# Squared-ReLU attention and a routed expert layer on one core: expert weights gathered at set blocks, and turned token rows written from another ring of buffers

## The chip, the cores and the metric

The kernel runs on one core of a Trainium2 chip. The metric is the time of one execution in device microseconds (us); a kernel's time is the median of its runs. A core has five engines that each work through a queue of their own, strictly in order: TensorE (PE, matmuls), VectorE (DVE), ScalarE (ACT), GpSimd (POOL) and SyncE (SP). They wait for one another through semaphores. SP and POOL also issue the transfers between device memory and the core's buffers; a gather or a scatter through a list of indices is issued by POOL.

## The reference

`u`, `v` are 8 x 2496 x 256, `z` is 8 x 2496 x 64, all of it f32. Attention has a squared ReLU in place of a softmax, and its result gates `u`; each of the 19968 tokens then goes to one of 8 experts.

```python
scores = scale * np.matmul(z, z.transpose(0, 2, 1))     # scale = 1 / 2496
attn = np.maximum(scores, 0.0) ** 2
x = (u * np.matmul(attn, v)).reshape(19968, 256)

logits = x @ w_gate                                     # 256 x 8
expert_idx = np.argmax(logits, axis=1)
gate_w = softmax(logits)[expert_idx]                    # of the chosen expert
for e in range(8):
    mask = expert_idx == e
    h = np.maximum(x[mask] @ w1[e], 0.0)                # 256 x 1024
    out[mask] = gate_w[mask, None] * (h @ w2[e])        # 1024 x 256
```

## The kernel before

**Precision.** A product of f32 operands is made of three matmuls: each operand is split into a rounded part ("hi", a cast on ACT) and a residual ("lo", a subtraction on DVE).

**Attention.** A step is (batch b, chunk c of up to 512 queries, pair kp of two blocks of 128 keys). `scores` (L311) runs three steps ahead: it makes the two key blocks' scores, squares them (L339, L340) into a buffer of the ring `tf` (`ring_f`, 3 buffers), casts (L319, L343) and subtracts (L320, L345, L349, L350). Scores that another chunk has in transposed form are read from there (L319, L320, and for half a chunk L335 to L338, through the buffers `rows`). `weighted` (L366, L368, L369) multiplies them with `v` into `acc0` and `acc1`. At a chunk's end `gate_x` (L383) multiplies by `u` and splits the result in three for the gate (L392 to L395); `turn_rows` transposes it (L407, into a buffer of the ring `th`, `ring_halves`, 3 buffers) and writes it out as token rows (L412); `route` (L438) finds each token's expert and its place in the expert's list (the products L471 and L473, then L480 to L487), and scatters entries there (L490, four per chunk).

**Expert tiles.** Tiles are counted from 0. The first eight ("A", 512 tokens each) take tokens of all batches but the last; two of them share the weights of an expert (`NA` = 4 pairs). The others are built from the rest of the lists. Weights are called (w, h): expert set w, half h, 1 MB each, gathered by `load_w` (L712) through an index column into one of six slots s0 to s5. One half holds two "pieces" (two blocks of the 1024 hidden features each), which `split_piece` (L746) turns into hi and lo: two casts on ACT (L762, L764) and two subtractions on DVE (L763, L765) a piece. The next steps for a tile i are

- `load_x` (L743): POOL gathers its token rows, 128 rows a gather, into a buffer of the ring `rows` (3 buffers);
- `turn_x` (L768): DVE transposes 32 x 32 squares of it into `sq` (L773), SP writes that to memory (L776, `far`) and reads it back with features on the partitions into `tp` (L778); `sq` and `tp` are both buffers of the ring `th`, and `sq` comes free when L776 has landed;
- `split_x` (L782): the cast L788 and the residual L789;
- per block of 128 hidden features `up` (six matmuls L809, then L813 on ACT and L814 on DVE) and `down` (six matmuls L835 to L837), eight blocks a tile; `up` runs two blocks ahead of `down`;
- `turn_y` (L850) transposes the result back, `finish` (L872) multiplies by the gate into a buffer of the ring `tf` (L879) and POOL scatters the rows to the output (L886).

**What sets the order.** The last batch's last chunks already start the expert tiles: the table `loads` names, by the number of steps left, what is issued there. In `tiles` (L1038) a tile's block 0 loads what comes later: the second half of the next set and the first half of the one after it, and the rows of tile i + 3; its middle block turns tile i + 2. The program's text is not the order on the engines. A scheduler places every instruction by a simulated timeline, as soon as it finds its operands and buffers free; only what is issued through `pinned` (L373) is put behind the instruction that was last issued on each engine. What is placed early in an engine's queue holds up all that stands behind it there.

Of the kernel before, what the change touches and what calls it, by code (L numbers as in the profile page):

```python
# [8 lines left out]
F32 = mybir.dt.float32  # L9
# [3 lines left out]
I32 = mybir.dt.int32  # L13
# [6 lines left out]
P = 128  # L20
KQ = 64
G, R = 4, 32
D = 256
# [31 lines left out]
def fused_kernel(ctx: ExitStack, tc: tile.TileContext, zt, ut, v, wg, wcat, out):  # L55
    nc = tc.nc
    B, _, SP = zt.shape
    S = SP - KQ
    NK = SP // P
    NKP = NK // 2  # L60
# [7 lines left out]
    NA = 4  # L68
# [10 lines left out]
    sb = ctx.enter_context(tc.tile_pool(name="sb", bufs=1))  # L79
# [8 lines left out]
    def ring_f():  # L88
        return sb.tile([P, 2, QC], F32, name="tf", tag="tf", bufs=3)
# [13 lines left out]
    def ring_halves():  # L103
        return sb.tile([P, 4, QC], U16, name="th", tag="th", bufs=3)
# [5 lines left out]
    def slot(i):  # L110
        return sb.tile([P, 2 * F], F32, name=f"s{i}", tag=f"s{i}")
# [157 lines left out]
    def turn(b, c, cc, h, a):  # L269
# [3 lines left out]
        else:  # L273
            tt = turned_.pop((b, c, cc))
        to = tt.rearrange("p (s t i k) -> p i t s k", s=G, t=4, i=4)[:, 2 * h:2 * h + 2]
        nc.vector.transpose(out=to, in_=a.rearrange("p i (t s k) -> p i t s k", t=4, s=G))  # L276
        if h:
# [3 lines left out]
    def bring(b, cc, c):  # L281

        d = kept_rows.pop((b, cc, c))
        st = slot(home["bring", b, cc, c])
        for q in range(G):
            nc.sync.dma_start(st[q * R:(q + 1) * R].rearrange("p (g e) -> p g e", g=G),
                              d.rearrange("(g q) (s e) -> s q g e", g=G, s=G)[q])
        brought[b, cc, c] = st.rearrange("p (g t i k) -> p t i g k", g=G, t=4, i=4)
# [84 lines left out]
    def pinned(work):  # L373

        last = {}
        for i in nc.cur_bb.bb.instructions[-400:]:
            last[i.engine] = i
        with ExitStack() as behind:
            for i in last.values():
                behind.enter_context(tc.issue_after(i))  # L380
            work()
# [296 lines left out]
    NF = F // P  # L678
# [18 lines left out]
    own = [t not in seconds[which] for which, t, _ in order]  # L697
    wof = [sum(own[:i + 1]) - 1 for i in range(NT)]
# [6 lines left out]
    lists, ents, xgs, pieces, turned, xts, yts = {}, {}, {}, {}, {}, {}, {}  # L705
    outs, kept = [], []

    def load_w(w, h):
        which, t, _ = order[first_of[w]]
        wr = slot(free[0])  # L710
        free.append(free.pop(0))
        nc.gpsimd.indirect_dma_start(out=wr, out_offset=None, in_=wcat,  # L712
                                     in_offset=bass.IndirectOffsetOnAxis(ap=lists[which]["widx"][:, h, t:t + 1], axis=0))
        weights[w, h] = wr

    by2, by4 = [lst.rearrange("(a k) w -> a (k w)", k=k) for k in (2, 4)]
# [1 line left out]
    def load_e(i):  # L718
        which, t, n = order[i]
        en = ents[i] = sb.tile([P, BS, ENT], F32, name="ent", bufs=9)  # L720
        to = en.rearrange("p s w -> p (s w)")
        eidx = lists[which]["eidx"]
        parts = [(by4, t, 0, BS)] if n == BIG else [(by2, t, 0, 2)]
        for s in range(2, blocks[i] if n < BIG else 0):
            parts.append((lst, lists[which][{384: 2, 448: 4, 480: 5}[n], s / 2] + t, s, s + 1))
        for src, at, a, z in parts:
            d = nc.gpsimd.indirect_dma_start(out=to[:, a * ENT:z * ENT], out_offset=None, in_=src,
                                             in_offset=bass.IndirectOffsetOnAxis(ap=eidx[:, at:at + 1], axis=0))
            if which == "A":
                firsts.append(d)  # L730
                for of, o in scatters:
                    if of == B - 1:
                        tc.declare_no_dep(d.ins, o.ins, reason="places of a later batch")
# [4 lines left out]
    def load_x(i):  # L738
        which, k = order[i][0], blocks[i]
        src = xrows[0:NTOK - S, :] if which == "A" else xrows  # L740
        xg = ring_rows()
        for s in range(k):
            nc.gpsimd.indirect_dma_start(out=xg[:, s, :], out_offset=None, in_=src, in_offset=token(i, s))  # L743
        xgs[i] = xg
# [23 lines left out]
    def turn_x(i):  # L768

        k = blocks[i]  # L770
        xg = xgs.pop(i)
        sq, tp = [ring_halves().rearrange("p a n -> p (a n)").bitcast(F32)[:, 0:k * D] for _ in range(2)]
        nc.vector.transpose(out=sq.rearrange("p (g i s t) -> p s g i t", g=G, i=2, s=k),  # L773
                            in_=xg[:, 0:k, :].rearrange("p s (g i d) -> p s g i d", g=G, i=2))
        far = dram.tile([P, F], F32, name="far", tag="far", bufs=4)
        nc.sync.dma_start(far[:, 0:k * D], sq)  # L776
        for g in range(G):
            nc.sync.dma_start(tp[g * R:(g + 1) * R].rearrange("p (a e) -> p a e", a=G),  # L778
                              far[:, g * k * 2 * R:(g + 1) * k * 2 * R].rearrange("(a p) e -> p a e", a=G))
        turned[i] = tp  # L780

    def split_x(i):  # L782

        k = blocks[i]
        tp = turned.pop(i).rearrange("p (a j t) -> p j a t", a=G, t=R)
        xh, xl = [x.rearrange("p i n -> p (i n)")[:, 0:k * D] for x in (ring_hi(), ring_lo())]
        h, l = [x.rearrange("p (j a t) -> p j a t", a=G, t=R) for x in (xh, xl)]
        nc.scalar.copy(h, tp)  # L788
        nc.vector.tensor_tensor(l, tp, h.bitcast(F32), op=ALU.subtract)  # L789
        xts[i] = [x.rearrange("p (i n) -> p i n", i=2) for x in (xh, xl)]  # L790

    def flat(i):
        return cols[i] != SMALL and i < NM - 3

    def up(gi):
        i, g = groups[gi]
        n = cols[i]
        w1 = pieces[piece_of[gi]][0]
        xh, xl = xts[i]
        ph = ps1.tile([P, QC], F32, name="ph", tag="ps1")  # L800
        m = fs_of[i]
        for c in range(m):
            f = g * m + c
            fs = slice(f % 2 * P, (f % 2 + 1) * P)
            o = ph[:, c * n:(c + 1) * n]
            p = 0
            for dd in range(2):
                for part, xx in ((0, xh), (0, xl), (1, xh)):
                    nc.tensor.matmul(o, lhsT=w1[:, part, dd, fs], rhs=xx[:, dd, :n], start=p == 0, stop=p == 5)  # L809
                    p += 1  # L810
        hh, hl = ring2(), ring2()
        m *= n
        nc.scalar.activation(hh[:, :m], ph[:, :m], AF.Relu)  # L813
        nc.vector.scalar_tensor_tensor(hl[:, :m], ph[:, :m], 0.0, hh[:, :m].bitcast(F32),  # L814
                                                     op0=ALU.max, op1=ALU.subtract)
        return hh, hl
# [150 lines left out]
    for work in (lambda: split_v(0, 0), lambda: split_z(0, 1), lambda: split_z(0, 2), lambda: prepare(0),  # L967
# [8 lines left out]
             NKP + 1: [lambda: load_w(0, 0)],  # L976
             NKP: [lambda: load_x(1)],
             NKP - 1: [lambda: load_w(0, 1)],
             NKP - 3: [lambda: load_w(1, 0)],
             NKP - 2: [lambda: turn_x(0)],  # L980
             1: [lambda: load_x(2), lambda: load_e(3)],
             0: [lambda: turn_x(1)]}
# [52 lines left out]
    n_pieces = LP + 1  # L1035
    hs.update({gi: up(gi) for gi in range(1, LU)})

    def tiles(lo, hi, n_pieces):  # L1038

        due = []  # L1040
        mine = [gi for gi, (i, _) in enumerate(groups) if lo <= i < hi]
        for gi in mine:
            i, g = groups[gi]
            G = NF // fs_of[i]
            if bg:
                pinned(bg.pop(0))
            if i == NM - 1 and g == 0:
                needed.append(nc.values_load(lists["F"]["ns"], min_val=0, max_val=NS))
            if g == 0:
                for w, h in ((wof[i] + 1, 1), (wof[i] + 2, 0)):  # L1050
                    if own[i] and w <= wof[hi - 1]:
                        load_w(w, h)
                if i + 3 < hi:
                    load_x(i + 3)
                if i + 4 < hi:
                    load_e(i + 4)
            ahead = min(gi + LU, mine[-1])
            while n_pieces < min(piece_of[ahead] + LP + 1, NPC * (wof[hi - 1] + 1)):
                split_piece(n_pieces)
                n_pieces += 1  # L1060
            if i + 2 < hi and g == G // 2:
                turn_x(i + 2)
            if i + 1 < hi and g == G - 3:
                pinned(lambda: split_x(i + 1))
            if gi + LU <= mine[-1]:
                hs[gi + LU] = up(gi + LU)
            down(gi, *hs.pop(gi))
            if due and gi == due[0][0]:
                pinned(lambda: finish(due.pop(0)[1]))
            if g == G - 1:  # L1070
                if flat(i):
                    turn_y(i)
                    due.append((gi + 8, i))
                elif i == NM - 1:
                    pinned(lambda: finish(i))
                else:
                    finish(i)
        assert not due
# [61 lines left out]
```

## Time and profile before

| | |
|---|---|
| median of 3 runs | 2202.89 us |
| lowest, highest | 2202.73, 2205.02 us |
| the profiled execution's own time | 2201.62 us |
| its span in the profile | 2199.5 us |
| mean granted TensorE clock | 0.998 |

The profiled execution lies 2.1 us above its span (launch and end) and 1.3 us below the median. Times in the profile count from the span's start. The attention takes the first 1300 us or so; the expert tiles' first product stands at 1302 us, among the last matmuls of the attention. In rows of the profile `s`, `t`, `th`, `tf` are names of buffer rings without their numbers; rows of an order have the number of each allocation (`tf_13563`), which tells them apart.

### The profile page before, as it was taken

The page shows a single profiled execution, that of the slowest core. Times are in us where ns is not written, and L with a number is a line of the kernel's source. Part 1 is how long each engine was busy: PE and PEld are TensorE (multiplying, and loading weights), DVE is VectorE, ACT ScalarE, POOL GpSimd, SP SyncE. Part 2 cuts the span into 40 slices and gives each one's busy share as a digit, 9 for nine tenths or more (in the row PEclk, how much of TensorE's full clock was granted, in tenths as well). Part 3 has the DMA queues.
Part 4 walks back from the last instruction along what each step waited for, and adds up shares of the span by engine and source line. Part 5 has one row for each costly group of instructions (what it writes and reads, how often), then busy time and mean ns, then how long its engine had stood idle before and what let it go on. Part 6 is the DMA issues. An engine that isn't in the chain of part 4 may idle for free.

```text
span 2199.5 us, 32283 instructions
## 1 busy us (share of the span) xinstructions
PE 2175.4 (99%) x11200; PEld 1833.6 (83%) x11200; DVE 1680.9 (76%) x2811; ACT 1320.8 (60%) x1833; POOL 713.1 (32%) x743
## 2 busy tenths in 40 slices
PE   9999999999999999999999999999999999999997
PEld 6888888888888888888888887888888898888886
DVE  9888888888888888888888878657667576665753
ACT  8657658657657667667667643446556464554543
POOL 3010120220210220210320463646556465565422
PEclk9999999999999999999999999999999999999999
DMA  7976866867867768757857795757867677786730
GB/s 246 270 187 210 243 175 215 242 170 219 237 168 249 221 163 250 224 171 232 237 157 220 200 294 183 231 185 227 270 221 254 209 244 245 242 254 222 256 129 33
DMA packets 302364, 473.22 MB, mean 215 GB/s; under 512 B 112606, under 2 KB 191906, under 8 KB 282224
## 3 DMA queue, kind: packets, MB, share of 16 engines
q1 hardware_dynamic: 268720, 347.20, 53.5%
q0 software_dynamic: 33472, 123.88, 17.4%
q8 instruction: 89, 1.46, 0.3%
q14 instruction: 83, 0.68, 0.1%
HBM read 286.15 MB, written 185.14 MB: 214 GB/s over the span
## 4 chain that ended last, share of the span: by engine, by line
PE 94%; DVE 2%; DMA 2%; issue 1%; POOL 0%; ACT 0%; SPq 0%; POOLq 0%; ACTq 0%; DVEq 0%
PE ph L809 19%; PE acc L366 16%; PE acc L369 16%; PE acc L368 15%; PE y L836 5%; PE y L837 5%; PE y L835 5%; PE ps_s L330 4%; PE ps_s L331 4%; PE y L844 2%; PE pt L421 1%; PE y L846 1%; DMA scr<-s 1%; POOL out_dram L886 0%; DMA far<-th 0%
## 5 line engine op out<-in xcount | busy, mean ns | idle before, releaser
L490 POOL DMA_INDIRECT lst<-gw,posi x160 | 189.9, 1187 | 865.9 <-DVE posi L487 486.0
L369 PE MATMUL acc<-thi,t 128*128 128x512 f32 (+1 forms) x1200 | 461.7, 386 | 0.0
L366 PE MATMUL acc<-thi,t 128*128 128x512 f32 (+1 forms) x1200 | 451.7, 386 | 0.7 <-DVE thi L343 0.7
L368 PE MATMUL acc<-tlo,t 128*128 128x512 f32 (+1 forms) x1144 | 442.6, 387 | 1.9 <-DVE tlo L345 1.5
L813 ACT ACTIVATE t<-ph 128x512 fp32r<-128x512 f32 (+3 forms) x328 | 191.2, 583 | 381.3 <-PE ph L809 361.0
L814 DVE SCALAR_TENSOR_TENSOR t<-ph,t 128x512 fp32r<-128x512 f32 (+3 forms) x328 | 218.7, 667 | 260.0 <-ACT t L813 259.3
L809 PE MATMUL ph<-thi,t 128*128 128x512 f32 (+4 forms) x1256 | 382.2, 357 | 0.6 <-DVE t L814 0.6
L339 ACT ACTIVATE tf<-ps_s 128x1024 f32<-128x1024 f32 (+1 forms) x240 | 226.9, 952 | 184.0 <-PE ps_s L331 183.6
L366 PEld LDWEIGHTS acc<-thi,t 128*128 128x128 f32 x1200 | 225.3, 188 | 41.8 <-DVE thi L343 1.2
L369 PEld LDWEIGHTS acc<-thi,t 128*128 128x128 f32 x1200 | 225.4, 188 | 40.3
L809 PEld LDWEIGHTS ph<-thi,t 128*128 128x128 f32 x1256 | 228.2, 188 | 34.0 <-DVE t L814 1.0
L368 PEld LDWEIGHTS acc<-tlo,t 128*128 128x128 f32 x1144 | 215.0, 188 | 41.3 <-DVE tlo L345 2.8
L276 DVE STREAM_TRANSPOSE s<-tf 128x1024 f32<-128x1024 f32 x160 | 197.2, 1234 | 55.4 <-ACT tf L340 55.1
L340 ACT ACTIVATE tf<-tf 128x1024 f32<-128x1024 f32 (+1 forms) x240 | 234.6, 987 | 5.9
L809 PE MATMUL ph<-tlo,t 128*128 128x512 f32 (+4 forms) x628 | 224.4, 358 | 2.9 <-DVE tlo L789 2.9
L886 POOL DMA_INDIRECT out_dram<-tf,ent x161 | 172.5, 1071 | 144.4 <-ACT tf L879 81.7
L743 POOL DMA_INDIRECT rows<-xrows,ent x161 | 164.4, 1021 | 117.4 <-DVE th L773 44.1
L345 DVE TENSOR_TENSOR tlo<-tf,thi 128x1024 fp32r<-128x1024 f32 (+1 forms) x168 | 190.0, 1132 | 15.4 <-ACT thi L343 15.0
L331 PE MATMUL ps_s<-t,t 128*128 128x512 f32 (+1 forms) x480 | 177.6, 373 | 0.2 <-DVE t L139 0.2
L343 ACT CAST thi<-tf 128x1024 fp32r<-128x1024 f32 (+2 forms) x162 | 158.9, 983 | 26.6 <-PE acc L369 22.0
L836 PE MATMUL y<-t,t 128*128 128x512 f32 (+3 forms) x448 | 170.7, 381 | 0.5 <-DVE t L814 0.5
L837 PE MATMUL y<-t,t 128*128 128x512 f32 (+3 forms) x448 | 170.4, 380 | 0.0
(269 smaller groups left out, 4234.0 us busy)
## 6 DMA issues: line engine op xcount, KB each, us to landing
scr<-s SPq DMA_DIRECT2D x80, 1024.0 KB
s<-scr SPq DMA_DIRECT2D x320, 256.0 KB
vr<-in_v_dram SPq DMA_DIRECT2D x80, 256.0 KB
u<-in_ut_dram SPq DMA_DIRECT2D x32, 512.0 KB
xrows<-th SPq DMA_DIRECT2D x128, 128.0 KB
far<-th SPq DMA_DIRECT2D x32, 512.0 KB
th<-far SPq DMA_DIRECT2D x128, 128.0 KB
fary<-x SPq DMA_DIRECT2D x30, 512.0 KB
```

The costliest lines, as they stand in the source:

```text
L276: nc.vector.transpose(out=to, in_=a.rearrange("p i (t s k) -> p i t s k", t=4, s=G))
L331: nc.tensor.matmul(ps[:, i, m:w], lhsT=hl_k, rhs=lh_q[:, m:w], start=False, stop=True)
L339: nc.scalar.activation(a[:, :, m:w], ps[:, :, m:w], AF.Relu)
L340: nc.scalar.activation(a[:, :, m:w], a[:, :, m:w], AF.Square)
L366: nc.tensor.matmul(acc[d][:, :n], lhsT=vh, rhs=hi[:, i, :n], start=first and i == 0, stop=False)
L368: nc.tensor.matmul(acc[d][:, :n], lhsT=vh, rhs=lo[:, i, :n], start=False, stop=False)
L369: nc.tensor.matmul(acc[d][:, :n], lhsT=vl, rhs=hi[:, i, :n], start=False, stop=last and i == 1)
L809: nc.tensor.matmul(o, lhsT=w1[:, part, dd, fs], rhs=xx[:, dd, :n], start=p == 0, stop=p == 5)
L813: nc.scalar.activation(hh[:, :m], ph[:, :m], AF.Relu)
L814: nc.vector.scalar_tensor_tensor(hl[:, :m], ph[:, :m], 0.0, hh[:, :m].bitcast(F32), op0=ALU.max, op1=ALU.subtract)
L836: nc.tensor.matmul(y, lhsT=wh, rhs=hl[:, :n], start=False, stop=False)
L837: nc.tensor.matmul(y, lhsT=wl, rhs=hh[:, :n], start=False, stop=g == NF - 1)
```

## The change

There are two edits. (1) `load_w` can be held: it first copies its index column with DVE to a small tile `due`, and the gather reads the copy, so that it can't be placed ahead of the copy. Six gathers are issued that way, each `pinned` at a set block of the first tiles: (1,0) at block 0 of tile 0, (1,1) at block 4 of tile 0, (2,0) and (2,1) at block 0 of tiles 1 and 2, (3,0) at block 4 of tile 2, (3,1) at block 0 of tile 4. The places where the same gathers were issued before go, (1,0) among them in the table `loads`. (2) `turn_x` takes `sq` from the ring `tf` in place of `th`; `tp` stays in `th`.

```diff
-    def load_w(w, h):
+    def load_w(w, h, held=False):
         which, t, _ = order[first_of[w]]
+        at_ = lists[which]["widx"][:, h, t:t + 1]
+        if held:
+            due_now = sb.tile([P, 1], I32, name="due", bufs=3)
+            nc.vector.tensor_copy(due_now, at_)
+            at_ = due_now
         wr = slot(free[0])
         free.append(free.pop(0))
         nc.gpsimd.indirect_dma_start(out=wr, out_offset=None, in_=wcat,
-                                     in_offset=bass.IndirectOffsetOnAxis(ap=lists[which]["widx"][:, h, t:t + 1], axis=0))
+                                     in_offset=bass.IndirectOffsetOnAxis(ap=at_, axis=0))
...
-        sq, tp = [ring_halves().rearrange("p a n -> p (a n)").bitcast(F32)[:, 0:k * D] for _ in range(2)]
+        sq = ring_f().rearrange("p a n -> p (a n)")[:, 0:k * D]
+        tp = ring_halves().rearrange("p a n -> p (a n)").bitcast(F32)[:, 0:k * D]
...
-             NKP - 3: [lambda: load_w(1, 0)],
...
+    held_w = {(0, 0): (1, 0), (0, NF // 2): (1, 1), (1, 0): (2, 0)}
+    for t in range(2, NA):
+        held_w[2 * t - 2, 0] = t, 1
+        if t + 1 < NA:
+            held_w[2 * t - 2, NF // 2] = t + 1, 0
...
+            if (i, g) in held_w:
+                pinned(lambda: load_w(*held_w[i, g], held=True))
...
-                    if own[i] and w <= wof[hi - 1]:
+                    if own[i] and NA <= w <= wof[hi - 1]:
                         load_w(w, h)
```

In the changed kernel the lines from L712 on have other numbers: the gather of weights is L717, the pieces L767 to L770, the row gather L748, the transposition L779, the split L794 and L795, `up`'s epilogue L819 and L820, the scatter L892.

The change moves instructions on three engines. On DVE, around the end of the last full chunk of the attention, the transpositions of tile 1 (`rows_13283`) and tile 2 (`rows_13538`, before `rows_13540`). The order before, where L395 belongs to that chunk and `s2_13350` is the last operand of the chunk after it:

```order
L395 TENSOR_TENSOR x2_13290<-x1_13289 128x1024
L320 TENSOR_TENSOR tlo_13326<-s5_13014,thi_13325 128x1024
L343 CAST s2_13350<-tf_13352 128x2x192
L763 TENSOR_TENSOR t4_13518<-s4_13265,t4_13518 128x512
L336 TENSOR_TENSOR s2_13350<-rows_13234,s2_13350 128x256
L338 TENSOR_TENSOR s2_13350<-rows_13234,s2_13350 64x256
L765 TENSOR_TENSOR t4_13519<-s4_13265,t4_13519 128x2x256
L349 TENSOR_TENSOR s2_13350<-tf_13352,s2_13350 128x192
L350 TENSOR_TENSOR s2_13350<-tf_13352,s2_13350 64x192
L427 TENSOR_REDUCE l_13298<-pt_13381 128x32
L320 TENSOR_TENSOR tlo_13408<-s3_13128,thi_13407 128x1024
L407 STREAM_TRANSPOSE th_13423<-x_13288 128x2x16x32
```

The same stretch in the changed kernel:

```order
L395 TENSOR_TENSOR x2_13290<-x1_13289 128x1024
L779 STREAM_TRANSPOSE tf_13563<-rows_13283 128x4x8x32
L779 STREAM_TRANSPOSE tf_13791<-rows_13538 128x4x8x32
L320 TENSOR_TENSOR tlo_13326<-s5_13014,thi_13325 128x1024
L343 CAST s2_13350<-tf_13352 128x2x192
L768 TENSOR_TENSOR t4_13516<-s4_13265,t4_13516 128x512
L336 TENSOR_TENSOR s2_13350<-rows_13234,s2_13350 128x256
L338 TENSOR_TENSOR s2_13350<-rows_13234,s2_13350 64x256
L770 TENSOR_TENSOR t4_13517<-s4_13265,t4_13517 128x2x256
L320 TENSOR_TENSOR tlo_13406<-s3_13128,thi_13405 128x1024
L407 STREAM_TRANSPOSE th_13421<-x_13288 128x2x16x32
L349 TENSOR_TENSOR s2_13350<-tf_13352,s2_13350 128x192
```

Both transpositions moved up: tile 1's stood twelve rows behind L395 (right behind L407), tile 2's 46 rows behind it. Tile 3's, which stood at the head of tile 1's residual L789, is now 19 rows behind L395, and tile 0's has moved back a little, behind the L487 of the chunk before.

On POOL, in the same stretch, the row gathers of tiles 1 to 6 and the gathers of weights (`in_wcat_dram`). First the order before, then the changed one; the table `loads` and the block 0 of the first tiles issue them:

```order
L490 DMA lst_73<-gw_12987,posi_13216 164352x16 x4
L743 DMA rows_13283<-xrows_72,ent_13067 128x256 x4
L743 DMA rows_13540<-xrows_72,ent_13198 128x256 x4
L712 DMA s1_13323<-in_wcat_dram,lawidx_11914 128x2048
L712 DMA s5_13379<-in_wcat_dram,lawidx_11914 128x2048
```

```order
L490 DMA lst<-gw,posi 164352x16 x4
L748 DMA rows<-xrows,ent 128x256 x8
L717 DMA s_13323<-in_wcat_dram,lawidx 128x2048
L748 DMA rows<-xrows,ent 128x256 x8
L402 MEMSET l 64x8
L748 DMA rows<-xrows,ent 128x256 x8
L717 DMA s_13626<-in_wcat_dram,due 128x2048
L490 DMA lst<-gw,posi 164352x16 x4
L717 DMA s_13762<-in_wcat_dram,due 128x2048
L490 DMA lst<-gw,posi 164352x16 x4
L717 DMA s_13976<-in_wcat_dram,due 128x2048
```

The gather of (1,0) (slot s5; `s_13626` in the second piece) moved from behind that of (0,1) to behind the row gathers of tiles 3 to 6. Before, the five gathers after it followed the rows of tiles 3 and 4 in one run, with no other row between them; now scatters L490 stand between the first of them, and scatters of the output and rows between the later ones.

On ACT, at tile 0's first blocks, the casts of the two pieces of (1,0). In the order before they read `s5_13379` and stand ahead of all of tile 0's L813; in the changed order:

```order
L819 ACTIVATE t2_13585<-ph_13578 128x512
L819 ACTIVATE t2_13620<-ph_13613 128x512
L819 ACTIVATE t2_13675<-ph_13668 128x512
L819 ACTIVATE t2_13699<-ph_13692 128x512
L767 CAST t4_13719<-s5_13626 128x512
L769 CAST t4_13720<-s5_13626 128x2x256
L767 CAST s0_13786<-s5_13626 128x512
L769 CAST s0_13786<-s5_13626 128x2x256
L819 ACTIVATE t2_13732<-ph_13725 128x512
```

They moved to between block 3 and block 4, and the subtractions that belong to them on DVE with them. On TensorE the sequence of matmuls is all but the same; the product of the placement (L471, L473) of the chunk before the last two stands eight matmuls earlier.

## Prediction

> **What bounds the kernel now.** First the engines' busy times, then TensorE's waits from 1260 us (the last chunk of the attention) to 2156 us.
>
> ```profile
> PE 2175.4 (99%) x11200; PEld 1833.6 (83%) x11200; DVE 1680.9 (76%) x2811; ACT 1320.8 (60%) x1833; POOL 713.1 (32%) x743
> PE ph L809 <- DVE tlo L789: 2.9, 1, 2.9
> PE y L836 <- DVE t L814: 0.5, 1, 0.5
> PE acc L368 <- DVE tlo L320: 0.4, 1, 0.4
> ```
>
> TensorE is busy 99% of the span and the change leaves its matmuls as they are. What can be won is its idle time near the change: 2.9 + 0.5 + 0.4 = 3.8 us, and nothing else in 900 us, the whole of the steady expert tiles included. What can be lost has no such limit. So the question is whether new waits outweigh 3.8 us.
>
> The long wait, in TensorE's, SyncE's and VectorE's rows of the timeline (start, duration, line, idle before):
>
> ```profile
> 1327.24 0.39 PE L835 MATMUL y<-t,t 128*128 128x512 f32 x1
> 1330.54 0.50 PE L809 MATMUL ph<-tlo,t 128*128 128x512 f32 x1 [2.91 <-DVE tlo L789]
> 1312.66 7.38 SPq L412 DMA_DIRECT2D xrows<-th  x4
> 1320.45 0.34 SPq L776 DMA_DIRECT2D far<-th  x1
> 1328.06 1.25 DVE L773 STREAM_TRANSPOSE th<-rows 128x1024 f32<-128x1024 f32 x1 [4.23 <-DMA far<-th]
> 1329.28 1.21 DVE L789 TENSOR_TENSOR tlo<-th,thi 128x1024 fp32r<-128x1024 f32 x1
> ```
>
> SyncE hangs in L412 until 1320.04, so tile 2's turned rows leave for memory only at 1320.45. Tile 3's transposition, which wants the `th` buffer they leave from, starts at 1328.06, and the residual of tile 1 (L789), for which TensorE stands, is behind it in VectorE's order.
>
> **The change part by part.** *Turned rows in `tf` buffers.* Tile 3's transposition no longer asks for tile 2's `th` buffer. In the new order it is issued some fifty rows earlier, and tile 1's residual has nothing late ahead of it: the 2.9 us go.
>
> But freed from `th`, the transpositions of tiles 1 and 2 now stand right behind L395, ahead of work that the last attention chunk needs. Before, this is what VectorE did from L395 on:
>
> ```profile
> 1281.36 1.22 DVE L395 TENSOR_TENSOR x<-x 128x1024 bf16<-128x1024 f32 x1
> 1284.69 1.23 DVE L320 TENSOR_TENSOR tlo<-s,thi 128x1024 fp32r<-128x1024 f32 x1 [2.12 <-ACT thi L319]
> 1285.84 0.35 DVE L343 CAST s<-tf 128x384 fp32r<-128x384 f32 x1
> 1286.11 0.68 DVE L763 TENSOR_TENSOR t<-s,t 128x512 fp32r<-128x512 f32 x1
> 1289.10 0.43 DVE L336 TENSOR_TENSOR s<-rows,s 128x256 fp32r<-128x256 f32 x1 [2.31 <-ACT s L335]
> 1289.54 0.46 DVE L338 TENSOR_TENSOR s<-rows,s 64x256 fp32r<-64x256 f32 x1
> 1290.03 0.69 DVE L765 TENSOR_TENSOR t<-s,t 128x512 fp32r<-128x512 f32 x1
> 1290.64 0.35 DVE L349 TENSOR_TENSOR s<-tf,s 128x192 fp32r<-128x192 f32 x1
> 1291.02 0.36 DVE L350 TENSOR_TENSOR s<-tf,s 64x192 fp32r<-64x192 f32 x1
> 1291.41 0.26 DVE L427 TENSOR_REDUCE l<-pt 128x32 f32<-128x96 f32 x1
> 1291.70 1.23 DVE L320 TENSOR_TENSOR tlo<-s,thi 128x1024 fp32r<-128x1024 f32 x1
> 1292.84 1.24 DVE L407 STREAM_TRANSPOSE th<-x 128x1024 f32<-128x1024 f32 x1
> 1294.00 1.20 DVE L773 STREAM_TRANSPOSE th<-rows 128x1024 f32<-128x1024 f32 x1
> ```
>
> TensorE wants the first L320's result at 1289.29, and at 1291.92 the chunk's last operand (`s2_13350` in the order), whose last writers are L349 and L350:
>
> ```profile
> 1289.29 0.36 PE L368 MATMUL acc<-tlo,t 128*128 128x448 f32 x1
> 1291.92 0.37 PE L368 MATMUL acc<-s,t 128*128 128x448 f32 x1
> ```
>
> VectorE works in order, so tile 2's transposition holds all of this back until tile 2's rows are gathered. GpSimd's gathers (scatters L490, then eight L743, four for tile 1 and four for tile 2; the last two rows below are the first and last of eight for tiles 3 and 4), and how long a gather of this stage takes to land:
>
> ```profile
> 1272.08 1.00 POOL L490 DMA_INDIRECT lst<-gw,posi  x1 [2.27 <-DMA xrows<-th]
> 1288.29 0.94 POOL L743 DMA_INDIRECT rows<-xrows,ent  x1 [0.30 <-DMA rows<-near]
> 1292.11 1.64 POOL L743 DMA_INDIRECT rows<-xrows,ent  x1 [0.17 <-ACT thi L319]
> 1303.46 1.09 POOL L743 DMA_INDIRECT rows<-xrows,ent  x1 [0.30 <-issue]
> DMA to landing us min/median/max: 2.8/5.1/7.8
> ```
>
> The scatters wait for a product (L471, L473) that stands eight matmuls earlier in the new order; at (1291.92 − 1289.29) / 13 = 0.20 us each between the two rows above, that is 1.6 us. The last gather of tile 2 then starts at 1286.7 and lands 2.8 to 5.1 us later, at 1289.5 to 1291.8. The transposition takes 1.2: it ends, call it t0, at 1290.7 to 1293.0. In the new order ten operations follow up to L350; by the starts above L320 1.15, L343 0.27, L768 (before L763) 0.61, L336 0.44, L338 0.49, L770 (L765) 0.61, the second L320 1.14, L407 1.16, L349 0.38, L350 0.39: 6.6 us. The operand is there at 1297.3 to 1299.6 instead of before 1291.92: **TensorE waits 5.4 to 7.7 us**. I take 6.6, a landing of about 4 us, since most of that row's 28 gathers went out in the crowd behind the weights and these don't. The 0.5 and 0.4 waits lie behind this one and go into it, as VectorE catches up while TensorE stands.
>
> [...]
>
> Tile 3's gathers start when L338 frees their buffer, at t0 + 3.2; four of them, at (1303.46 − 1292.11) / 7 = 1.6 us each, and a landing of 5.1 put the rows there at t0 + 13.1. VectorE gets to its transposition at about t0 + 10.5 and waits 2.6 us; the residuals behind it are wanted late enough. With 7.8 us of landing some 2 us would reach TensorE. I take 0.
>
> *Held weights.* Six copies of 128x1 on VectorE: the nearest rows are its small ones such as L427's 0.26 us, so under 1.6 us in all, each while TensorE has some 3 us of queued work: 0. The gather of (1,0) now comes behind sixteen row gathers (tiles 3 to 6): they end at t0 + 3.2 + 16 × 1.25 to 1.6 = t0 + 23.2 to 28.8 (1.25 is 0.95 and the 0.30 between two in the rows above). Its landing, the casts of its two pieces, and where TensorE wants what is queued behind them on ScalarE (block 4 of tile 0: its first L835; the row ahead of it is block 3's):
>
> ```profile
> DMA to landing us min/median/max: 5.6/7.2/11.8
> 1305.56 0.61 ACT L764 CAST s<-s 128x512 fp32r<-128x512 f32 x1
> 1306.08 0.59 ACT L813 ACTIVATE t<-ph 128x512 fp32r<-128x512 f32 x1
> 1318.38 0.39 PE L835 MATMUL y<-t,t 128*128 128x512 f32 x1
> 1321.10 0.39 PE L835 MATMUL y<-t,t 128*128 128x512 f32 x1
> ```
>
> Landing 5.6 to 7.2, four casts 4 × 0.52, then block 4's L819 0.6 and L820 0.7: 9.0 to 10.6 us behind the issue, t0 + 32.2 to 39.4. TensorE wants it at 1321.10; with 1291.92 moved to t0 + 6.6 that is t0 + 35.8. So from 3.6 early to 3.6 late; the middle is on time, and as only lateness counts I take 0.7. The next held gathers are set four blocks apart and are wanted as far apart, 4 × 2.72 = 10.9 us by the two L835 rows; one gather and four scatters lie between on GpSimd, five times about 1.25: none is tighter than the first.
>
> **Sum.** 2201.62 (the profiled execution) + 6.6 + 0.7 − 3.8 = 2205.1. The median of the runs shown is 1.3 above that execution, so **2206.4 us** against 2202.89: 3.5 us slower, which is less than 0.2% (4.4 us), about what a measurement of this kernel can tell from no change. From 5.4 + 0 to 7.7 + 3.6 the same sum gives 2204.5 to 2210.4.
>
> **Rivals.** *Tile 2 is no obstacle.* If its rows land as VectorE gets there (1281.36 + 1.22 and two transpositions, 1285.0), the operand comes at 1291.6 and nothing is lost: −3.8, 2199.1, the largest gain I can see and still short of 0.2%. Against it stand twelve GpSimd DMAs at 1.25 us or more from 1270.5: even so the last starts at 1284.2 and lands, 2.8 us later, at 1287.0, which costs 2.9 us and gives 2202.0. Chance 0.2; only with something that I don't see it passes 0.2% faster: 0.07.
>
> *The (1,0) weights decide.* Landing 11.8 us at the late end of the issue, they come 8.2 us late, and everything queued on ScalarE behind the cast stops TensorE: 2202.89 + 6.6 − 3.8 + 8.2 = 2213.9. It decides, for a gather issued at t0 + 26, from a landing of 35.8 − 26 − 3.4 = 6.4 us on. For it: ScalarE and VectorE both run in order, and the casts stand ahead of block 4. Chance 0.13.
>
> *The `tf` ring in the steady tiles.* There it is shared with the finished rows on their way out; the transposition is issued about ten blocks (2.72 us each) ahead of its split instead of twenty, at the least four, 10.9 us.
>
> ```profile
> L778 SPq EVENT_SEMAPHORE  x44: 17/2303/9488, 1333.5 to 2109.1; - x44
> ```
>
> The chain in between is 1.2 + 0.34 (L776), a wait of 2.3 us in the middle and 9.5 at most (L778's row), a landing (bounded by the gathers' 5.1) and the residual, 1.2: 10.1, or 17.3 at the worst. One tile that is 6.4 late costs that: 2212.8. Chance 0.1.
>
> *TensorE's clock falls.* By the steps above it would stand 3.8 us at 1289.29 and 2.8 more at 1291.92. The longest idle stretch here, and the one after it (window, engines' busy times, granted clock, DMA share):
>
> ```profile
> 1327.00:1330.60 3.60, 0.69 (x4) 0.25 (x2) 2.54 (x4) 0.00 (x0) 2.98 (x3) 1.00 0.43 121
> 1330.60:1334.00 3.40, 3.40 (x15) 2.83 (x16) 2.07 (x11) 1.45 (x3) 2.60 (x3) 1.00 0.68 233
> ```
>
> After 2.9 us of idling the clock was 1.00. If it halved for 3.4 us as the second window is long, 1.7 us would be added: 2208.1. [...] Chance 0.07.
>
> **How the numbers follow.** The forecast's own case has the rest, 0.5; about a third of it lies above 2207.3. Faster by over 0.2%: 0.07. Slower: 0.17 from the forecast's case, 0.13 + 0.1 + 0.04 from the rivals, 0.44. Within 0.2%: 0.49. The range takes in most of the first rival below and of the late weights above: 2200.5 to 2212.0.
>
> **What would show it.** Right: in the changed profile TensorE waits for `tlo` L320 or the chunk's last operand near 1290, VectorE sits idle before the second of two adjacent L779 for rows of L748, and the 2.9 us wait for L795 is gone. Wrong: no idle time of TensorE between 1285 and 1300, or waits at each expert tile. A wait of TensorE in tile 0's block 4, for L819 or L820 behind casts of (1,0), speaks for the late weights, a granted clock under 1.00 for the last rival.

## The result and the profile after

| | kernel before | changed kernel |
|---|---|---|
| median of 6 runs each | 2202.81 us | 2217.28 us |
| lowest, highest | 2201.32, 2205.14 us | 2211.28, 2218.55 us |
| the profiled execution's own time, its span | 2201.62, 2199.5 us | 2218.27, 2216.5 us |
| mean granted TensorE clock | 0.998 | 0.994 |

The ratio is 1.0057, with a 95% interval of 1.0047 to 1.0067: by it the change costs some 12.6 us (the medians lie 14.5 us apart, and the two profiled executions 16.7), and the time lies above the range that was given. The drift below is that of the two profiled executions. TensorE all but keeps its sequence, so the n-th matmul of one trace is the n-th of the other, and the difference of their starts (below: the drift) says where the time went: +6.6 us at the matmul that starts at 1296.1 in the changed trace, +8.7 at 1300.4, +4.8 at 1335.3, +7.6 at 1691.0, +9.9 at 1838.3, +11.9 at 1842.2, +15.4 at 1858.7, +16.8 at the end. So 8.7 us are lost at the place that the prediction named, 3.9 won back behind it as forecast, and 12.0 lost in the steady tiles, where it had put a chance of 0.1.

TensorE's waits of the changed kernel from 1260 to 2170 us (line, what it waited for: us, times, longest):

```profile
PE acc L368 <- DVE tlo L320: 6.4, 1, 6.4
PE y L842 <- DVE t L820: 4.8, 2, 2.9
PE ph L815 <- ACT thi L794: 2.0, 1, 2.0
PE ph L815 <- DVE tlo L795: 0.3, 1, 0.3
```

The waits of 2.9, 0.5 and 0.4 us of before are gone. The first row is the wait near 1290; the next two are new and are in three expert tiles.

**The early wait.** VectorE, GpSimd and TensorE in the changed kernel's timeline, and how long the 13 row gathers from 1266 to 1296 took to land:

```profile
1281.55 1.21 DVE L395 TENSOR_TENSOR x<-x 128x1024 bf16<-128x1024 f32 x1
...
1293.72 1.25 DVE L779 STREAM_TRANSPOSE tf<-rows 128x1024 f32<-128x1024 f32 x1 [8.35 <-DMA rows<-xrows,ent]
1294.89 1.18 DVE L320 TENSOR_TENSOR tlo<-s,thi 128x1024 fp32r<-128x1024 f32 x1
...
1301.00 0.36 DVE L350 TENSOR_TENSOR s<-tf,s 64x192 fp32r<-64x192 f32 x1
...
1286.39 0.94 POOL L748 DMA_INDIRECT rows<-xrows,ent  x1 [0.30 <-issue]
...
1296.13 0.74 PE L368 MATMUL acc<-tlo,t 128*128 128x448 f32 x1 [6.38 <-DVE tlo L320]
...
DMA to landing us min/median/max: 5.8/6.1/7.4
```

Tile 2's last gather goes out at 1286.39, VectorE stands 8.35 us in front of that tile's transposition, and L320's residual, which TensorE wants at 1289.7, comes right behind it. That is the picture of the forecast, with a longer landing.

**The clock.** Between 1270 and 2200 us the changed kernel's trace has three stretches at half clock: from 1293.80 for 6.83 us, from 1839.93 for 3.42 and from 1857.00 for 3.41. The rows below show each with the 3.41 us ahead of it, the first stretch in two parts, and the wait of 2.89 us that ends at 1690.97 with what follows it (window, its length, busy us of PE, PEld, DVE, ACT and POOL, then the granted clock, the DMA share and GB/s):

```profile
1290.39:1293.80 3.41, 0.00 (x0) 0.00 (x0) 0.08 (x1) 1.34 (x2) 2.60 (x3) 1.00 1.05 401
1293.80:1297.21 3.41, 1.08 (x3) 1.00 (x4) 3.41 (x5) 0.00 (x0) 1.67 (x2) 0.50 0.93 351
1297.21:1300.63 3.42, 3.42 (x11) 2.84 (x9) 3.38 (x5) 0.36 (x1) 2.88 (x2) 0.50 1.01 242
...
1687.00:1691.00 4.00, 1.11 (x6) 0.59 (x4) 3.50 (x6) 1.25 (x3) 3.09 (x4) 1.00 1.00 393
1691.00:1694.50 3.50, 3.50 (x15) 2.90 (x16) 3.50 (x6) 1.94 (x5) 2.89 (x3) 1.00 0.44 117
...
1836.52:1839.93 3.41, 1.35 (x4) 0.68 (x5) 1.63 (x2) 2.71 (x5) 0.37 (x1) 1.00 1.04 362
1839.93:1843.35 3.42, 3.42 (x11) 2.84 (x10) 3.42 (x7) 2.35 (x5) 2.51 (x4) 0.50 0.65 246
...
1853.59:1857.00 3.41, 1.49 (x6) 1.24 (x7) 2.46 (x4) 0.42 (x1) 2.50 (x4) 1.00 0.84 334
1857.00:1860.41 3.41, 3.41 (x9) 2.67 (x8) 2.22 (x3) 0.60 (x1) 2.50 (x4) 0.50 0.38 82
```

After three of the four waits (6.38, 2.89, 2.05 and 1.96 us in order of time) the granted clock goes from 1.00 to 0.50, at the first still within the wait, at the third and fourth 1.6 and 1.5 us behind its end: for 6.83 us at the first (2.3 us of them are still the wait, so they cost half of the 1.08 + 3.42 us of work, 2.2) and for 3.4 us each at the third and fourth (half of it, 1.7 each), 5.6 us in all. That is an estimate: it takes a matmul to last twice as long at 0.50. By the drift it is 2.1 from 1296.1 to 1300.4, 1.6 from +10.8 at 1839.9 to +12.4 at 1843.4 and 1.6 from +14.6 at 1857.0 to +16.2 at 1860.4. Around the second wait, 2.89 us, and behind it the clock is 1.00, though that wait is longer than the third and the fourth. What decides which wait is followed by half clock is not shown.

**The steady tiles.** What VectorE waited for in front of L779 from 1340 to 2200 us (us, times), and the two places where that wait reached TensorE:

```profile
  DMA out_dram<-tf,ent: 31.9, 8
```

```profile
1687.51 1.25 DVE L779 STREAM_TRANSPOSE tf<-rows 128x1024 f32<-128x1024 f32 x1 [6.45 <-DMA out_dram<-tf,ent]
...
1690.97 0.50 PE L842 MATMUL y<-t,t 128*128 128x512 f32 x1 [2.89 <-DVE t L820]
...
1853.24 1.25 DVE L779 STREAM_TRANSPOSE tf<-rows 128x1024 f32<-128x1024 f32 x1 [4.66 <-DMA out_dram<-tf,ent]
...
1855.51 0.50 PE L842 MATMUL y<-t,s 128*128 128x512 f32 x1 [1.96 <-DVE t L820]
```

Eight transpositions stand until a scatter of finished rows has left the `tf` buffer that they want. Before, in the same window, VectorE waited for nothing in front of a transposition. The epilogue L820 of the block at hand stands behind it, and for that TensorE stands.

At 1838.3 it is another thing: the tile's turned rows come late. Its transposition, the reading back, the cast and the matmul:

```profile
1818.67 1.24 DVE L779 STREAM_TRANSPOSE tf<-rows 128x1024 f32<-128x1024 f32 x1
...
1829.02 1.77 SPq L784 DMA_DIRECT2D th<-far  x4
...
1837.22 1.04 ACT L794 CAST thi<-th 128x1024 fp32r<-128x1024 f32 x1 [5.12 <-DMA th<-far]
...
1838.32 0.51 PE L815 MATMUL ph<-thi,t 128*128 128x512 f32 x1 [2.05 <-ACT thi L794]
```

The same tile's transposition and cast in the kernel before:

```profile
1787.91 1.25 DVE L773 STREAM_TRANSPOSE th<-rows 128x1024 f32<-128x1024 f32 x1
...
1824.31 1.05 ACT L788 CAST thi<-th 128x1024 fp32r<-128x1024 f32 x1
```

From the transposition's start to the cast's it was 36.4 us, with time to spare; now it is 18.6, every microsecond of it chain, and TensorE waits. Over all tiles from 8 on it was 36 to 67 us before and is 11 to 49 now. Waits and half clock in the steady tiles come to 2.9 + 2.0 + 2.0 + 0.3 + 1.7 + 1.7 = 10.6 of the 12.0 us; the rest lies in small steps that I did not follow.

While the first four experiments ran, all kernels took some 3% longer (the kernel before 2271.94 us; ScalarE idles 60 to 76 us in front of `up`'s epilogue for something that the profile doesn't show) and scattered by about 1%, so of those runs the waits are used more than the ratios, and two later runs, of 3627.49 us (experiment 9) and 5807.91 us (the kernel before), are in no ratio.

### The profile page after: what moved, and what is told of

The parts are those of the page before. It is cut to its first block, busy times and chain, and to the rows that moved or that the text cites. A ratio compares the mean times of both kernels' runs of the same rounds, so it can differ in the third digit from the quotient of the medians.

```text
span 2216.5 us, 32319 instructions
## 1 busy us (share of the span) xinstructions
PE 2183.4 (99%) x11200; PEld 1838.1 (83%) x11200; DVE 1678.5 (76%) x2817; ACT 1321.2 (60%) x1833; POOL 725.7 (33%) x743
## 5 line engine op out<-in xcount | busy, mean ns | idle before, releaser
L490 POOL DMA_INDIRECT lst<-gw,posi x160 | 200.4, 1252 | 849.0 <-DVE posi L487 477.6
L368 PE MATMUL acc<-tlo,t 128*128 128x512 f32 (+1 forms) x1144 | 443.6, 388 | 7.3 <-DVE tlo L320 6.4
L819 ACT ACTIVATE t<-ph 128x512 fp32r<-128x512 f32 (+3 forms) x328 | 191.4, 584 | 377.6 <-PE ph L815 362.4
L820 DVE SCALAR_TENSOR_TENSOR t<-ph,t 128x512 fp32r<-128x512 f32 (+3 forms) x328 | 218.6, 668 | 246.3 <-ACT t L819 245.8
L368 PEld LDWEIGHTS acc<-tlo,t 128*128 128x128 f32 x1144 | 215.5, 188 | 47.0 <-DVE tlo L320 6.8
L892 POOL DMA_INDIRECT out_dram<-tf,ent x161 | 176.5, 1096 | 182.5 <-ACT tf L885 113.2
L345 DVE TENSOR_TENSOR tlo<-tf,thi 128x1024 fp32r<-128x1024 f32 (+1 forms) x168 | 190.9, 1137 | 15.4 <-ACT thi L343 14.9
L748 POOL DMA_INDIRECT rows<-xrows,ent x161 | 169.2, 1051 | 83.2 <-issue 38.6
L842 PE MATMUL y<-t,t 128*128 128x512 f32 (+3 forms) x448 | 170.7, 381 | 2.9 <-DVE t L820 2.9
L319 ACT CAST thi<-s 128x1024 fp32r<-128x1024 f32 x104 | 109.1, 1049 | 103.2 <-PE acc L369 100.5
```

The source lines that it names most:

```text
L345: nc.vector.tensor_tensor(lo[:, :, m:n], a[:, :, m:n], hi[:, :, m:n].bitcast(F32), op=ALU.subtract)
L368: nc.tensor.matmul(acc[d][:, :n], lhsT=vh, rhs=lo[:, i, :n], start=False, stop=False)
L490: i = nc.gpsimd.indirect_dma_start(out=lst, out_offset=bass.IndirectOffsetOnAxis(ap=posi[:m, j:j + 1], axis=0), in_=gw[:m, j, :], in_offse ...
L842: nc.tensor.matmul(y, lhsT=wh, rhs=hl[:, :n], start=False, stop=False)
```

## The experiments

A line's number can differ by a few between these kernels; each is named by what it is. All ratios are against the kernel before, with their 95% intervals.

**1. The held weights alone** (`sq` in `th` as before):

```diff
-        sq = ring_f().rearrange("p a n -> p (a n)")[:, 0:k * D]
-        tp = ring_halves().rearrange("p a n -> p (a n)").bitcast(F32)[:, 0:k * D]
+        sq, tp = [ring_halves().rearrange("p a n -> p (a n)").bitcast(F32)[:, 0:k * D] for _ in range(2)]
```

> The held weights alone; the squares stay in the ring th. Theory A (all of the loss is the ring tf: tile 2's transposition placed early, 8.7 us with the clock that falls behind it, and the steady tiles' transpositions that wait for finished rows, 12 us): no wait near 1290 us, no wait of L779's successor for the output's scatters, no halved clock; the 2.9 us wait at tile 1 shrinks, since the five weights no longer go out in one run: 2199 to 2203 us. Theory B (the later gathers of weights and what they push on the queues are the loss): 2210 to 2217 us, with waits of TensorE behind casts of weights.

Measured: 0.9991 [0.9965, 1.0018]. There is no wait of more than 0.6 us near 1290, and the transpositions wait for nothing. The held weights make neither of the losses.

**2. The ring alone** (`sq` in `tf`; weights gathered where they were before: `load_w` without `held`, `held_w` out, (1,0) back in `loads`, and `if own[i] and w <= wof[hi - 1]:`).

> The squares in the ring tf alone; weights gathered as before. Theory A: as the whole change, 2211 to 2218 us, TensorE standing about 6 us near 1290 us for L320 and 2 to 3 us at each of some steady tiles whose transposition waits for the output's scatters. Theory B: within 3 us of the kernel before, 2200 to 2206 us.

Measured: 1.0047 [1.0019, 1.0075]. TensorE waits 6.3 us in front of L368, the drift there is +9.1, and +4.9 at 1336, as in the whole change. In front of the transpositions VectorE waits, from 1340 on (us, times):

```profile
  DMA out_dram<-tf,ent: 22.5, 7
```

Both losses come with the ring.

**3. and 4. The ring in the early tiles alone, and in the later ones alone** (weights held in both):

```diff
-        sq = ring_f().rearrange("p a n -> p (a n)")[:, 0:k * D]
+        sq = (ring_f().rearrange("p a n -> p (a n)") if i < 8
+              else ring_halves().rearrange("p a n -> p (a n)").bitcast(F32))[:, 0:k * D]
```

and the same with `i >= 8`.

> Both edits, but tiles 8 and later keep th for their squares. Theory A: the early place of tile 2's transposition costs 8.7 us less the 3.9 us that are won, and nothing after it: 2205 to 2209 us, no wait after 1340 us. Theory B: as the whole change, 2211 to 2218 us.

> Both edits, but tiles 0 to 7 keep th for their squares. Theory A: the steady tiles' part alone, up to 12 us: 2207 to 2214 us, no wait near 1290 us, waits of 2 to 3 us after 1600 us with an L780 ahead of them that waits for the output's scatters. Theory B: as the whole change.

Measured: 0.9963 [0.9936, 0.9989] and 1.0068 [1.0042, 1.0094]. The early kernel waits 7.2 us for L320 and its transpositions wait for no scatter; the later one waits 14.7 us, in six of them, for scatters. The places are as expected, but the early kernel's ratio below 1 doesn't fit its own wait of 7.2 us; experiments 10 and 11 run the two again.

**5. The whole change with only tile 2's transposition kept at its place in the text:**

```diff
-                turn_x(i + 2)
+                if i == 0:
+                    pinned(lambda: turn_x(2))
+                else:
+                    turn_x(i + 2)
```

> Both edits, but tile 2's turn is put behind what was last issued on each engine, so that its transposition stands behind the last chunk's work again (and tile 3's right behind it). Theory A: the wait of some 6.5 us near 1290 us and the halved clock behind it go, 8.7 us; the steady tiles' waits stay: 0.1 to 0.5% slower than the kernel before, against 0.57% for the whole change. Theory C (the early wait comes from the shared ring or from the rows' late landing wherever the transposition stands): the wait stays or moves on by a few us, 0.5 to 0.7% slower.

Measured: 2211.89 us against 2202.61, 1.0046 [1.0032, 1.0059]. The wait near 1290 is gone and the drift at 1328 is −2.9; at the end it is +9.8. TensorE's two longest rows from 1260 on, and VectorE's wait in front of the transpositions:

```profile
PE y L842 <- DVE t L820: 5.1, 4, 2.5
PE ph L815 <- ACT thi L794: 2.7, 1, 2.7
```

```profile
  DMA out_dram<-tf,ent: 31.8, 8
```

So the early wait is made by where tile 2's transposition stands (tile 3's moved along with it, right behind): the ring and the held weights are as before, and the wait is gone. The steady tiles lose their 12 us without it.

**6. Held weights, and the ring for tile 3 alone** (`if i == 3` in the diff of 3.).

> Held weights, and only tile 3's squares in tf; all others in th. Theory A: neither of the two losses, and the 2.9 us wait gone: 0 to 0.2% faster than the kernel before, no transposition that waits for the output's scatters. If held weights cost something by themselves, it is not faster.

Measured: 2199.33 us against 2202.61, 0.999 [0.9981, 0.9999]: a little faster than both kernels. What TensorE waits for from 1260 to 2170:

```profile
PE ph L816 <- DVE t L821: 0.6, 1, 0.6
PE ph L816 <- DVE x L392: 0.3, 1, 0.3
```

The 2.9 us that the change could win, and nothing lost.

**7. The whole change with a fourth `tf` buffer** (the ring `vr` gives up one of its four for the room):

```diff
-        return sb.tile([P, 2, QC], F32, name="tf", tag="tf", bufs=3)
+        return sb.tile([P, 2, QC], F32, name="tf", tag="tf", bufs=4)
-        return sb.tile([P, 2, D], F32, name="vr", bufs=4)
+        return sb.tile([P, 2, D], F32, name="vr", bufs=3)
```

> Both edits, with a fourth tf buffer (and three in place of four for raw rows of v in the attention, to make room). The order of the transpositions on VectorE stays that of the whole change. Theory A: the wait near 1290 us stays, 8.7 us with the clock; the transpositions' waits for the output's scatters, 32 us on VectorE in the changed kernel, fall under 5 us, and TensorE's 3 waits behind them go: 0.1 to 0.3% slower than before. If the steady loss came from where the transpositions stand rather than from the buffers, it stays at 0.5% and more.

Measured: 2218.71 us, 1.0069 [1.0055, 1.0083]. The waits for scatters fall to 9.3 us in two, yet the drift still goes from +7.1 at 1337.7 to +19.3 at the end, with TensorE's waits in the same three tiles:

```profile
PE acc L368 <- DVE tlo L320: 8.1, 1, 8.1
PE y L842 <- DVE t L820: 5.3, 2, 3.3
PE ph L815 <- ACT thi L794: 2.1, 1, 2.1
```

The expectation fails. A fourth buffer is no cure: most of the idle time that VectorE spent on scatters goes, and what reaches TensorE stays. The two waits that are left, 3.0 us at 1689.4 and 6.3 at 1856.9, are just those in front of TensorE's two waits for L820, and they too are waits for a `tf` buffer; whether still more buffers would end them was not tried.

**8. Experiment 1 again.**

> The held weights alone once more, since the first chip's runs spread by over 1%. Theory A: within 0.2% of the kernel before, most of the 2.9 us wait gone; Theory B: 0.5% slower.

Measured: 2203.45 us against 2202.61, 1.0009 [1.0000, 1.0018]. The drift is −4.6 at 1326, so the early waits go, but it is +0.4 at the end. Most of it is given back around 1348, where the first piece of (2,0), the third held gather (issued at 1338.03), comes late:

```profile
1347.26 0.62 ACT L767 CAST t<-s 128x512 fp32r<-128x512 f32 x1 [6.34 <-DMA s<-in_wcat_dram,due]
...
1348.43 0.50 PE L840 MATMUL y<-t,t 128*128 128x512 f32 x1 [1.85 <-ACT t L818]
```

```profile
1350.40:1353.80 3.40, 3.40 (x9) 2.63 (x9) 3.40 (x8) 0.44 (x1) 0.00 (x0) 0.50 0.22 93
```

A wait of 1.85 us and half clock for 3.4 us, 1.7: 3.6 us. This is the forecast's rival of late weights, two gathers later; the whole change, which reaches this point with a drift of +4.6 instead of −4.1, has no wait of TensorE there.

**9. The ring for tile 3 alone, weights as before** (2.'s weights with 6.'s `i == 3`).

> Weights as before; only tile 3's squares in tf. The 2.9 us wait came from the th buffer that tile 3's transposition waited for: if that buffer is its cause, it goes here without any held weights, 0.05 to 0.2% faster than the kernel before. If the run of five weights is its cause, it stays, same time.

Measured: 2200.56 us against 2203.22, 0.999 [0.9981, 0.9999]. The 2.9 us go without the held weights too; the longest wait left from 1260 on is 1.2 us.

**10. and 11. Experiments 3 and 4 again.**

> The early transposition's part alone, on another chip: 8.7 less 3.9 us, 0.1 to 0.3% slower than the kernel before, TensorE standing 6 to 8 us near 1290 us with the clock at a half behind it, nothing after 1340 us. If the steady tiles' loss were a consequence of the early one, it would be here too: 0.5%.

> The steady part alone, on another chip: 0.3 to 0.6% slower, waits of TensorE only near 1680, 1830 and 1850 us, each behind a transposition that waits for the output's scatters or that is late for its split; 15 to 32 us of such waits on VectorE.

Measured: 2205.87 us, 1.0012 [1.0004, 1.0021], and 2215.79 us, 1.0062 [1.0043, 1.0081], against 2203.22. The early kernel has the wait near 1290,

```profile
PE acc L368 <- DVE tlo L320: 5.9, 1, 5.9
```

and a drift of +8.9 that is +4.5 at 1335. The profiled execution loses 3.8 us more at 1569, where nothing was expected: ScalarE stands 4.8 us for turned-back results (`yt`), and TensorE 1.2 us behind it; where the other 2.6 us go is not shown. That execution lies 3.8 us above the median, which fits with most runs not having it. The later kernel has −3.6 at 1327 and then climbs to +13.2, with VectorE's waits

```profile
  DMA out_dram<-tf,ent: 35.7, 9
  DMA far<-tf: 4.8, 1
```

Experiment 3's gain doesn't come again and is dropped. By the medians the early part costs 2.6 us and the later one 12.6; the held weights, 0.8 by experiment 8, are in both, so the two together would cost 14.4 us, and the whole change costs 12.6 (10.4 to 14.8 by its interval).

**12. A buffer of its own for the later tiles' `sq`**, shared with nothing (from tile 8; earlier tiles in `th`; `vr` with 3 for the room):

```diff
-        sq = ring_f().rearrange("p a n -> p (a n)")[:, 0:k * D]
+        sq = (sb.tile([P, 2, QC], F32, name="sq").rearrange("p a n -> p (a n)") if i >= 8
+              else ring_halves().rearrange("p a n -> p (a n)").bitcast(F32))[:, 0:k * D]
```

> As the run before, but the squares of tiles 8 and later have one buffer of their own, which no finished rows use (three in place of four buffers for raw rows of v make room). If sharing tf with the finished rows is the steady loss, in the place it gives the transposition or in the wait for the scatters, nothing of it is left: within 0.2% of the kernel before, no transposition waits for the output. If the loss came from leaving th alone, it stays at 0.3% and more.

Measured: 2273.53 us against 2203.22, 1.0313 [1.0293, 1.0332], the slowest of all by its ratio. VectorE's waits in front of the transpositions, one of them with the matmul that it holds up, and what TensorE waits for:

```profile
  DMA rows<-xrows,ent: 169.8, 36
  DMA far<-sq: 2.9, 2
```

```profile
1549.94 1.25 DVE L780 STREAM_TRANSPOSE sq<-rows 128x1024 f32<-128x1024 f32 x1 [8.52 <-DMA rows<-xrows,ent]
...
1551.75 0.74 PE L843 MATMUL y<-t,t 128*128 128x448 f32 x1 [5.21 <-DVE t L821]
```

```profile
PE y L843 <- DVE t L821: 43.3, 19, 5.4
```

The expectation fails, and shows what it is about. The profiled execution's mean granted clock is 0.987 over 2271.8 us, against 0.998 over 2199.5 before: by estimate, with 0.50 for all that is below 1.00, some 59 us of half clock against some 9. With a buffer that is nearly always free, the scheduler puts nearly every transposition right behind the gathers of its rows, before they have landed: the mistake of tile 2, in 36 places. From a transposition's start to its tile's cast it is now mostly 86 to 124 us (before 36 to 67). So the shared `th` ring had not been in the way: as it seems, it had held the transpositions back to a place where their rows had landed.

**13. and 14. Place and buffer apart:** every later transposition kept at its place in the text, once with 12.'s own buffer, once with the whole change's ring.

```diff
-                turn_x(i + 2)
+                pinned(lambda: turn_x(i + 2))
```

> The kernel with an own buffer for the squares of tiles 8 and later, but every turn in the expert tiles is put behind what was last issued on each engine, at its tile's middle block. Theory D (the loss is the place: a transposition that no buffer holds back is put right behind its row gathers, before they have landed, and VectorE stands): the 170 us of waits for gathers go, within 0.3% of the kernel before. Theory E (the own buffer, or leaving th, costs by itself): 2 to 3% slower as without the set place.

> The whole change, with the same set places for the turns. The order of the transpositions is that of the run before, and only the buffers differ. Theory D: no early wait near 1290 us, waits for the output's scatters under 10 us on VectorE, within 0.3% of the kernel before. Theory F (sharing tf with the finished rows costs wherever the transposition stands): some 30 us of waits for scatters, 0.4 to 0.6% slower.

Measured: 2217.30 us, 1.0058 [1.0044, 1.0071], and 2232.27 us, 1.0125 [1.0109, 1.0140], against 2204.02. VectorE's waits in front of the transpositions with the own buffer:

```profile
  DMA far<-sq: 3.4, 3
  DMA rows<-xrows,ent: 0.3, 1
```

and with the ring:

```profile
  DMA far<-tf: 1.5, 1
```

The place made the waits: of 169.8 us for gathers 0.3 are left, and of 31.9 us for scatters none. But neither kernel is at the 0.3% that a good place was to give. This place is too late: ScalarE's casts wait for the turned rows, and TensorE for the casts; with the own buffer

```profile
ACT thi L795 <- DMA th<-far: 37.7, 13, 8.7
```

```profile
PE ph L816 <- ACT thi L795: 6.4, 3, 4.2
PE y L851 <- ACT t L820: 4.4, 1, 4.4
```

and with the ring

```profile
PE ph L815 <- ACT thi L794: 16.5, 3, 6.6
```

(before: not one wait of that kind). The wait of 4.4 us for L820 is of the same making: the epilogue stands behind a cast that ScalarE had waited 8.7 us for. From the transposition's start to the cast's it is 12.8 to 35.5 us with the own buffer. Why the ring loses 0.67% more at the same places, by as many but longer waits of TensorE, stays open.

## Why the prediction was wrong

**Right, and what carried it.** TensorE's sequence stays, the three waits go (3.9 us for the 3.8), and tile 2's transposition, moved ahead of L320, holds the attention's last chunk up: a wait of 6.4 us where 6.6 was taken. Its last gather starts at 1286.39 (forecast 1286.7). The gather of (1,0) costs nothing (0.7 taken):

```profile
1317.71 0.94 POOL L717 DMA_INDIRECT s<-in_wcat_dram,due  x1 [4.18 <-DVE posr L485]
```

that is t0 + 22.7 (t0, the end of tile 2's transposition, is 1294.97), just ahead of the forecast's 23.2 to 28.8, and no wait of TensorE follows. That the two times meet is luck. The sixteen row gathers did not wait for L338, as was forecast; they began at 1288.89, 6.1 us ahead of t0 instead of 3.2 behind it, and were through at 1313.5. GpSimd then stood the 4.2 us of the row for the index column, which VectorE copied only at 1317.30.

**The 6.4 was partly right by accident.** The landing was taken as 4 us, since these gathers were thought to be out of the crowd; the row shows 5.8 at the least, and tile 2's last took 7.3 to the transposition. So t0 is 1294.97 and not 1290.7 to 1293.0, and the first wait 6.4 instead of 3.8. The second, 2.8 us for the chunk's last operand, did not come, because at half clock TensorE got there only at 1301.02, when L349 was just through (1300.97). At the forecast's 0.20 us a matmul it would have been there at 1298.8 and stood some 2.2 us, so the half clock's 2.2 us took the place of this wait. Together it is 8.7 us at 1300.4 against 6.6, and the term that was too small is the landing (5.8/6.1/7.4 in the row).

**The clock** had a chance of 0.07 and 1.7 us; it came three times, 5.6 us, of which the first 2.2 only replaced a wait. The 3.4 us that the forecast took for it were the length of a window that ran at 1.00; the changed trace has 0.50 for 3.41, 3.42 and 6.83 us. The argument against it, a 2.9 us wait at clock 1.00, was one case taken for a bound: in the changed kernel 2.89 us was followed by 1.00 as well, but 2.05 and 1.96 us were followed by 0.50. So the length of the wait alone does not tell; what does is not shown.

**The step that failed** is the rival "the `tf` ring in the steady tiles", chance 0.1, one tile, 6.4 us. The forecast's own sum has nothing for it, and it costs 12.0; without it the time would have come out in the range, as experiment 10 shows with 2205.87 us. The prediction priced the chain from transposition to residual (10.1 us, 17.3 at the worst) against the time that is left for it, and there it was short: the chain of the transposition at 1818.67 takes 1.2 us for itself, 9.1 to L784 and 8.2 from there to the cast, 18.6 before the residual. The 9.1 lies within its bound of 9.5; the reading back, taken as 5.1, took 8.2. That part costs 4.0 of the 12.0 us, 2.0 + 0.3 of waits and 1.7 of half clock. The rest comes from what was left out, the transposition's own place: 2.9 + 2.0 of waits and 1.7 of half clock are traced to it, 6.6 us. A buffer that comes free at another time lets the scheduler put the transposition elsewhere in VectorE's order, and there VectorE stands for a transfer, with the epilogues behind it: 31.9 us in eight waits, of which two reach TensorE. The prediction had seen exactly this for tile 2 and asked it of no other tile; "nothing else in 900 us", read from the kernel before, was taken as a property of the tiles, and was one of the old order.

**What is shown and what is not.** Shown: the ring makes both losses (1, 2, 8, 11); the early one is tile 2's place alone (5); VectorE's waits come and go with the place (12, 13, 14), and a fourth buffer leaves those that reach TensorE (7). Not shown: a place that keeps the ring and loses nothing in the steady tiles; the one that was tried is too late. Argued: that the scheduler moves the transpositions because in its simulated time the rows have landed, and the finished rows have left, sooner than on the chip. Open: 1.4 us of the steady loss, and the difference between 13 and 14.

## What to carry to other kernels

Where a scheduler places instructions as soon as it finds their buffers free, a shared ring is also a brake: before giving an operation another buffer, look at where it will then stand in its engine's order, which transfers it will stand for there, and what is queued behind it, and ask that of every instance, not only of the one with the visible wait. Moving the one tile that had the wait (experiments 6 and 9) won its 0.1%; moving all of them cost 0.57%. A place had two sides here: too early, VectorE stood for the transfer in (169.8 us in experiment 12); too late, ScalarE stood for the turned rows to come back (37.7 us in experiment 13).

## What the runs showed of the hardware

- TensorE's granted clock was 0.50 for 3.42 us after a wait of 2.05 us, for 3.41 after one of 1.96, and for 6.83 from within one of 6.38; it stayed 1.00 after one of 2.89, and after one of 2.91 in the kernel before. At 0.50 nine matmuls fell in the 3.41 us from 1857.00, at 1.00 seventeen in the 3.59 us behind it. So each of the two waits of 2 us cost some 1.7 us more by the estimate, and 1.6 by the drift.
- A gather of 128 rows, 128 KB, took 5.8 to 7.4 us to land at 1266 to 1296 us (share of the DMA engines 0.97 from 1286 to 1294), and 3.1/5.1/7.1 us in the same stage of the kernel before (share 0.81). Why is not shown.
- Reading a tile's turned rows back took 8.2 us from issue to the cast that stands for them, more than the median of a 1 MB gather of weights in the kernel before (5.6/7.2/11.8).
